# Selective attention and a SwiGLU block in one kernel: two of four head pairs of the second batch transposed by DMA over a DRAM scratch, two on TensorE

## The chip, the cores and the metric

The kernel runs on one core of a Trainium2 chip. A core has TensorE for matrix products, VectorE, ScalarE and GpSimd (POOL in the profile) for elementwise work, SyncE (SP) which here only issues DMAs, and 16 DMA engines that move data between DRAM and the on-chip memory. Each engine takes its instructions in order. Engines wait for each other by semaphores. Products of TensorE land in PSUM, which has eight banks here, and another engine must copy them out.

The metric is the time of one execution on the device in microseconds (us). The time before is the median of six runs.

## The reference

Causal attention with a bias from a running sum, then a gated feed-forward block over all tokens:

```python
scores = scale * np.matmul(q, k.transpose(0, 1, 3, 2))      # q, k, v: (8, 8, 576, 64)
cum = np.cumsum(np.maximum(s, 0.0), axis=-1)
bias = -(cum[:, :, :, None] - cum[:, :, None, :])
scores = np.where(causal, -1000000000.0, scores + np.minimum(bias, 0.0))
attn = softmax(scores)
x = np.matmul(attn, v).transpose(0, 2, 1, 3).reshape(B * S, H * D)   # (4608, 512)
g = x @ w_gate
out = (g * sigmoid(g) * (x @ w_val)) @ w_out                         # d_ff = 1536
```

## The kernel before

There are 64 heads (8 batches of 8), numbered through; head 8 is the first of batch 1. Heads are handled in groups of four for the keys and queries (group 4 is heads 16 to 19) and in pairs for the result (pair 4 is heads 8 and 9, the first pair of batch 1).

**Attention.** For a head, `score_piece` (line 344) makes the scores in four pieces on TensorE (line 367), ScalarE takes the exponential into `pt` (line 380), and POOL masks the diagonal (lines 383 and 388). `av_piece` (line 395) multiplies with the values (line 405); a column of ones gives the sum, and `av_out` divides on VectorE (lines 421 and 422) into `ot`, a tile of 128 tokens by 5 chunks by the 128 columns of a pair. Three `ot` tiles rotate.

**From ot to XT.** The feed-forward block needs x with the columns on the partitions, in `XT`, a ring of three token tiles of 512 tokens. There are two ways. `x_pe` (line 448) transposes the five chunks of a pair on TensorE (line 455) into a PSUM bank, and VectorE copies it to `XT` (line 462; ScalarE in batch 0, line 460). `x_out` (line 438) stores `ot` to a DRAM scratch `XS`, issued by POOL (line 439), and later `x_in` (line 443) has SP issue a transposing DMA from there into `XT` (line 446):

```python
def x_out(pr):
    nc.gpsimd.dma_start(
        XS[pr].rearrange("(c p) d -> p c d", p=128), ots.pop(pr)
    )

def x_in(pr):
    b, r = divmod(pr, H // 2)
    for lo, hi, at in x_parts(b):
        nc.sync.dma_start_transpose(XT[:, r, at : at + hi - lo], XS[pr][lo:hi])
```

Batches 0 and 1 take the first way, batches 2 to 7 the second.

**Keys and queries.** `load_qk` loads a group (line 152, SP), `cast_one` casts it to 16 bit (line 249 on POOL). Groups 0 to 4 are transposed on TensorE: `prep_one` calls `pe_transpose` (line 291) and `pe_out` (lines 318 and 320). From group 5 on (`NPE = 5`) they too go over DRAM: `scratch` stores the casts to `ks` and `qs` (line 263, SP), `transposes` loads them transposed into `pk` and `pq` (line 273, SP), and `split` copies them into `KQ` on VectorE (line 278).

**The order of work.** It is written out by hand. `first_batch` does batch 0. Then nine token tiles of the feed-forward block run (`ffn_items`: gate product line 571, value product line 586, output product line 620), and after each of their 36 items `pump` runs the generator `attn_items` up to a position that grows with the item number. In `attn_items` step kk emits the scores of head kk; `side` adds the loads, casts and scratch transfers of later groups after the second piece, and `PREP_AT` names the places of the TensorE transposes of the keys and queries of groups 3 and 4. After the scores of step kk come, in this order, the transposes named by `X_AT`, and then the products and divisions named by `AV_AT`. For batch 1, step 12 divides heads 8 and 9, step 13 transposes pair 4 and divides heads 10 and 11, step 14 transposes pair 5. The casts of group 4 are emitted at the start of step 13, and the first TensorE transpose of its keys after the fourth score piece of step 13. On SP the loads of group 6 come in step 12, and the scratch stores of group 5 in step 15.

The first token tile of the feed-forward block reads tokens of batch 0 alone; the second, tokens 512 to 1023, reads all four pairs of batch 1 as well.

The lines that choose the way are these three conditions: the set of scratch tiles (line 84), the choice between `x_pe` and `x_in` (line 541), and the call of `x_out` (line 554).

Of the kernel before, what the change touches and what calls it, by code (L numbers as in the profile page):

```python
# [13 lines left out]
BF16 = mybir.dt.bfloat16  # L14
# [5 lines left out]
def kernel(  # L20
# [14 lines left out]
    B, H, S, D = q.shape  # L35
    NT, DM = out.shape
    DF = moe_w_gate.shape[1]
    BH = B * H
    NCH = 5
# [24 lines left out]
    def pt_col(tj, bi):  # L64
# [12 lines left out]
    dram = ctx.enter_context(  # L77
        tc.tile_pool(name="dram", bufs=1, space=bass.MemoryType.DRAM)
    )

    NPE = 5
    XB = 2
    KS = {i: dram.tile([NR * S, 128], BF16, name=f"ks{i}") for i in range(NPE, NHB)}
    XS = {
        i: dram.tile([NCH * 128, 128], BF16, name=f"xs{i}") for i in range(XB * H // 2, BH // 2)
    }
    QS = {i: dram.tile([NR * S, 128], BF16, name=f"qs{i}") for i in range(NPE, NHB)}

# [17 lines left out]
    with tc.manual_schedule():  # L106
# [78 lines left out]
        def aug(hb, engs):  # L185
            for hh in range(HB):
                r, e = divmod(hh, 2)
                r0 = 64 * (1 - r)
                bh = hb * HB + hh
                engs[hh].dma_start(  # L190
                    KQ[hb % 2][r][r0 : r0 + 4, :, e * S : (e + 1) * S],
                    HL[bh : bh + 1, :, :, :],
                )
# [48 lines left out]
        def cast_one(hb, name, eng):  # L242
            cts[name, hb] = cp.tile([128, J, NR, D], BF16, tag="c" + name, bufs=2, name="c" + name)
            dst = cts[name, hb].rearrange("x j r d -> x r j d")
            src_t = loaded[name, hb]
            if eng is nc.scalar:
                nc.scalar.copy(dst, src_t)
            else:
                eng.tensor_copy(dst, src_t)
# [145 lines left out]
        def av_piece(bh, bis):  # L395
            b, h = divmod(bh, H)
            if bis[0] == 0:
                bs = take()
                avs[bh] = (view(bs, NCH * (D + 1)), bs)
            av = avs[bh][0]  # L400
            pt = pts[bh]
            for bi in bis:
                for tj in range(bi + 1):
                    c0 = pt_col(tj, bi)
                    nc.tensor.matmul(  # L405
                        av[:, bi * (D + 1) : (bi + 1) * (D + 1)],
                        pt[:, c0 : c0 + 128],
                        VT[b % 2][:, tj, h, :],
                        start=(tj == 0),
                        stop=(tj == bi),  # L410
                    )

        def av_out(bh):
            pr, e = divmod(bh, 2)
            if e == 0:
                ots[pr] = otp.tile([128, NCH, 2 * D], BF16, tag="ot", name="ot")
            ot = ots[pr]
            av, bs = avs.pop(bh)
            av3 = av.rearrange("p (c e) -> p c e", e=D + 1)
            rc = small.tile([128, NCH], FP32, tag="rc", name="rc")  # L420
            nc.vector.reciprocal(rc, av3[:, :, D])  # L421
            nc.vector.tensor_mul(  # L422
                ot[:, :, e * D : (e + 1) * D],
                av3[:, :, 0:D],
                rc[:, :, None].to_broadcast([128, NCH, D]),
            )
            give(bs)
            pts.pop(bh)
# [9 lines left out]
# [10 lines that stand above are left out]
        def x_pe(pr, eng=None):  # L448
            b, r = divmod(pr, H // 2)
            ot = ots.pop(pr)  # L450
            bs = take()
            ps = view16(bs, S)
            for c in range(NCH):
                n = 128 if c < 4 else TAIL
                nc.tensor.transpose(
                    ps[:, c * 128 : c * 128 + n], ot[0:n, c, :], ident[0:n, 0:n]
                )
            for lo, hi, at in x_parts(b):
                if eng is nc.scalar:
                    nc.scalar.copy(XT[:, r, at : at + hi - lo], ps[:, lo:hi])  # L460
                else:
                    nc.vector.tensor_copy(XT[:, r, at : at + hi - lo], ps[:, lo:hi])
            give(bs)

        def side(h, step):
            bh = HB * h + step
            if bh == H + 3:
                for c in range(5):
                    cast_v(1, c, nc.gpsimd)
            if h >= 3 and h + 3 < NHB and step == 0:  # L470
                load_qk(h + 3)
            if h + 1 < NHB and h + 1 >= NPE:
                if step == 0:
                    transposes(h + 1)
                    aug(h + 1, GP4)
                if step == 2:
                    split(h + 1, "k", nc.vector)
                if step == 3:
                    split(h + 1, "q", nc.vector)
            if h + 2 < NHB and h + 2 >= NPE:  # L480
                if step == 1:
                    cast_one(h + 2, "k", nc.gpsimd)
                if step == 2:
                    cast_one(h + 2, "q", nc.gpsimd)
                if step == 3:
                    scratch(h + 2)
            bn = h // 2 + 1
            if 2 <= bn < B:
                if h % 2 == 0:
                    if step == 2:  # L490
                        load_v(bn, (0, 1))
                    if step == 3:
                        load_v(bn, (2, 3, 4))
                else:
                    if step == 1:
                        cast_v(bn, 0, nc.gpsimd)
                        cast_v(bn, 1, nc.gpsimd)
                    if step == 2:
                        cast_v(bn, 2, nc.gpsimd)
                        cast_v(bn, 3, nc.gpsimd)  # L500
                    if step == 3:
                        cast_v(bn, 4, nc.gpsimd)

        def prep_one(hb, i):
            g, nm = divmod(i, 2)
            nm = ("k", "q")[nm]
            pe_transpose(hb, nm, g)
            for r in range(2):
                pe_out(hb, nm, g, r, nc.scalar if nm == "k" else nc.vector)
# [12 lines left out]
        def attn_items():  # L522
            for kk in range(H, BH + 2):
                h, step = divmod(kk, HB)
                if kk < BH:
                    if step == 1 and 3 < h + 1 < NPE:
                        cast_one(h + 1, "k", nc.gpsimd)
                        cast_one(h + 1, "q", nc.gpsimd)
                    if step == 0 and 3 < h + 1 < NPE:
                        aug(h + 1, GP4)  # L530
                    for ci in range(4):
                        score_piece(kk, ci)
                        if ci == 1:
                            side(h, step)
                        yield kk + 0.1 + ci / 8
                        if (step, ci) in PREP_AT.get(h, ()):
                            prep_one(h + 1, PREP_AT[h][step, ci])
                            yield kk + 0.1 + ci / 8
                for x in X_AT.get(kk, (kk - 2,)):
                    if x % 2 == 1 and H <= x < BH:  # L540
                        if x < XB * H:
                            x_pe(x // 2)
                            yield kk + 0.5
                        else:
                            x_in(x // 2)
                for p in AV_AT.get(kk, (kk - 1,)):
                    if H <= p < BH:
                        av_piece(p, (0, 1, 2))
                        yield kk + 0.6
                        av_piece(p, (3,))  # L550
                        yield kk + 0.7
                        av_piece(p, (4,))
                        av_out(p)
                        if p >= XB * H and p % 2 == 1:
                            x_out(p // 2)
                        yield kk + 0.8

# [159 lines left out]
        first_batch()  # L717
        second_psum()
        at = attn_items()
        state = {"pos": float(H)}  # L720

# [57 lines left out]
```

The softmax here doesn't subtract the row's maximum and nothing guards it: scores larger than these inputs give would overflow.

## Time and profile before

| what | value |
|---|---|
| median of six runs | 389.79 us (388.37 to 390.64) |
| the profiled execution: its time | 390.23 us |
| the profiled execution: span from first to last instruction | 388.5 us |
| granted clock of TensorE, mean | 0.998 |
| DMA queue of SP (q1) | 90816 packets, 45.36 MB, 49.4% of 16 engines |
| DMA queue of POOL (q0) | 9680 packets, 18.32 MB, 17.9% |
| transposes of x on TensorE, line 455 | 40 (20 in batch 0, 20 in batch 1) |
| copies of them on VectorE, line 462 | 4, 452 to 458 ns each |
| stores to `XS`, line 439 | 24, 862 to 951 ns each on POOL, 2.7 to 7.0 us to landing |
| transposing loads from `XS`, line 446 | 32, median 1138 ns each on SP |

The profiled execution's time is longer than its span by 1.7 us, which lie before the first and after the last instruction. The rows of the page give an engine's busy time, the 40 slices show it in tenths over the span, each slice 9.7 us long. In a timeline a row is the start and duration in us, the engine, the line, the operation, and what it writes and reads. An idle time in square brackets names what ended it. A row with SPq is a DMA issued by SP, its duration the time of issuing alone.

### The profile page before, as it was taken

What the parts mean: (1) busy time and instruction counts of PE and PEld (TensorE: products, weight loads), DVE (VectorE), ACT (ScalarE), POOL (GpSimd) and SP (SyncE); (2) the same over time, 40 slices, a digit from 0 to 9 for tenths busy, and PEclk for the clock granted to TensorE, in tenths of its full rate; (3) what the DMA queues carried; (4) which work ended last, traced back from release to release, by engine and by line L of the source; (5) the groups of instructions that cost most, each with busy time, mean ns of one, the idle gap of its engine ahead of it and who ended that gap; (6) DMA issues with size and microseconds to landing.
All of it is one profiled execution on the core that took longest, in us unless ns stands there. A gap on an engine that the chain in (4) does not pass through costs nothing.

```text
span 388.5 us, 7949 instructions
## 1 busy us (share of the span) xinstructions
PE 371.8 (96%) x3006; PEld 206.9 (53%) x3006; DVE 241.6 (62%) x431; ACT 214.4 (55%) x411; POOL 192.9 (50%) x329
## 2 busy tenths in 40 slices
PE   3779999999999999999999999999999999999995
PEld 2666556655555555555555555555555544444443
DVE  7666787458854786369735884588347625733750
ACT  7586787666646565566556555565465513323321
POOL 7584368565795766566656666576342220011001
PEclk9999999999999999999999999999999999999999
DMA  7999999996859998995789758964231222002002
GB/s 242 202 242 262 197 259 255 310 258 163 174 159 249 288 216 220 214 265 153 181 218 278 133 181 142 291 156 98 61 113 35 32 73 68 3 27 81 2 13 96
DMA packets 100535, 64.18 MB, mean 165 GB/s; under 512 B 81889, under 2 KB 85825, under 8 KB 100497
## 3 DMA queue, kind: packets, MB, share of 16 engines
q1 hardware_dynamic: 90816, 45.36, 49.4%
q0 software_dynamic: 9680, 18.32, 17.9%
q8 instruction: 23, 0.38, 0.4%
q14 instruction: 16, 0.12, 0.1%
HBM read 37.90 MB, written 19.86 MB: 149 GB/s over the span
## 4 chain that ended last, share of the span: by engine, by line
PE 82%; DVE 6%; DMA 5%; issue 3%; ACT 2%; POOL 0%; DVEq 0%; ACTq 0%; SPq 0%; POOLq 0%
PE bank L571 21%; PE bank L620 21%; PE bank L586 20%; PE bank L367 9%; PE bank L405 6%; DMA pk<-ks 2%; PE wide L367 2%; DVE pp L578 2%; ACT pt L380 1%; DVE ht L591 1%; DVE kq L320 1%; DMA kq<-HL 1%; PE one L405 1%; DMA XT<-xs 1%; DMA s_sb<-in_s_dram 1%
## 5 line engine op out<-in xcount | busy, mean ns | idle before, releaser
L380 ACT ACTIVATE pt<-bank 128x512 bf16<-128x512 f32 x224 | 104.2, 504 | 40.3 <-PE bank L367 26.6
L578 DVE SCALAR_TENSOR_TENSOR pp<-th,bank 128x512 bf16<-128x512 bf16 x108 | 74.1, 686 | 70.3 <-ACT th L576 69.5
L571 PE MATMUL bank<-XT,wg 128*128 128x512 bf16 x432 | 111.0, 379 | 1.2 <-DMA XT<-xs 0.6
L586 PE MATMUL bank<-XT,wv 128*128 128x512 bf16 x432 | 110.9, 379 | 0.0
L576 ACT ACTIVATE th<-bank 128x512 bf16<-128x512 f32 x108 | 64.5, 597 | 77.6 <-PE bank L571 73.3
L620 PE MATMUL bank<-wo,ht 128*128 128x512 bf16 x420 | 102.4, 379 | 0.0
L591 DVE TENSOR_TENSOR ht<-pp,bank 128x512 bf16<-128x512 bf16 x108 | 74.0, 685 | 8.8
L367 PEld LDWEIGHTS <-kq 128*128 128x128 bf16 x576 | 46.9, 100 | 39.4 <-issue 5.6
L367 PE MATMUL bank<-kq 128*128 128x128 bf16 (+4 forms) x504 | 65.9, 240 | 0.4 <-DVE ht L591 0.2
L383 POOL TENSOR_SCALAR_AFFINE_SELECT pt<-pt 128x512 bf16<-128x512 bf16 x64 | 41.2, 644 | 35.8 <-ACT pt L380 35.2
L571 PEld LDWEIGHTS <-wg 128*128 128x128 bf16 x432 | 38.3, 98 | 36.4 <-issue 1.0
L586 PEld LDWEIGHTS <-wv 128*128 128x128 bf16 x432 | 38.5, 98 | 34.9 <-issue 0.8
L620 PEld LDWEIGHTS <-ht 128*128 128x128 bf16 x420 | 37.1, 98 | 34.4
L405 PEld LDWEIGHTS <-pt 128*128 128x128 bf16 x960 | 41.5, 98 | 20.7
L439 POOL DMA_DIRECT2D xs<-ot x24 | 21.8, 910 | 58.5 <-DVE ot L422 58.5
L634 POOL DMA_DIRECT2D out_dram<-ysb x35 | 19.6, 562 | 60.9 <-ACT ysb L628 60.9
L628 ACT ACTIVATE ysb<-bank 128x512 f32<-128x512 f32 x35 | 20.9, 597 | 40.9 <-PE bank L620 39.8
L405 PE MATMUL bank<-vt,pt 128*128 128x65 bf16 x840 | 42.8, 194 | 0.0
L190 POOL DMA_DIRECT2D kq<-HL x52 | 31.3, 602 | 2.3 <-PE bank L571 1.6
L421 DVE RECIPROCAL rc<-bank 128x5 f32<-128x5 f32 x56 | 10.6, 190 | 34.4 <-PE bank L405 34.4
L422 DVE TENSOR_TENSOR ot<-bank,rc 128x320 bf16<-128x320 f32 x56 | 27.5, 492 | 1.9
L388 POOL TENSOR_SCALAR_AFFINE_SELECT pt<-pt 128x64 bf16<-128x64 bf16 x64 | 16.9, 264 | 21.2 <-ACT pt L380 21.1
(68 smaller groups left out, 213.7 us busy)
## 6 DMA issues: line engine op xcount, KB each, us to landing
out_dram<-ysb POOLq DMA_DIRECT2D x35, 256.0 KB, 3.1
rawk<-in_k_dram SPq DMA_DIRECT2D x15, 576.0 KB
rawq<-in_q_dram SPq DMA_DIRECT2D x15, 576.0 KB
rawv<-in_v_dram SPq DMA_DIRECT2D x32, 256.0 KB
xs<-ot POOLq DMA_DIRECT2D x24, 160.0 KB, 3.7
ks<-ck SPq DMA_DIRECT2D x11, 288.0 KB
qs<-cq SPq DMA_DIRECT2D x11, 288.0 KB
wg<-in_moe_w_gate_dram POOLq DMA_DIRECT2D x2, 768.0 KB, 11.5
```

Source lines behind the costliest of these rows:

```text
L190: engs[hh].dma_start(KQ[hb % 2][r][r0 : r0 + 4, :, e * S : (e + 1) * S], HL[bh : bh + 1, :, :, :],)
L367: nc.tensor.matmul(sc[:, o : o + w], T[:, 1, e * S + 128 * tj : e * S + 128 * (tj + 1)], T[:, 0, e * S + lo : e * S + hi], start=True, sto ...
L380: nc.scalar.activation(pt[:, c0 : c0 + W], sc[:, 0:W], AF.Exp, scale=0.125)
L383: nc.gpsimd.affine_select(pt[:, 1088:1600], pt[:, 1088:1600], pattern=[[0, 4], [1, 128]], compare_op=ALU.is_ge, fill=zreg, base=0, channel ...
L405: nc.tensor.matmul(av[:, bi * (D + 1) : (bi + 1) * (D + 1)], pt[:, c0 : c0 + 128], VT[b % 2][:, tj, h, :], start=(tj == 0), stop=(tj == bi),)
L422: nc.vector.tensor_mul(ot[:, :, e * D : (e + 1) * D], av3[:, :, 0:D], rc[:, :, None].to_broadcast([128, NCH, D]),)
L571: nc.tensor.matmul(pg, WG[j][:, c, f0 : f0 + 128], xt[:, c, :], start=(c == 0), stop=(c == 3),)
L576: nc.scalar.activation(th, pg, AF.Tanh, scale=0.5)
L578: nc.vector.scalar_tensor_tensor(pp, in0=th, scalar=1.0, in1=pg, op0=ALU.add, op1=ALU.mult)
L586: nc.tensor.matmul(pv, WV[j][:, c, f0 : f0 + 128], xt[:, c, :], start=(c == 0), stop=(c == 3),)
L591: nc.vector.tensor_mul(ht, pp, pv)
L620: nc.tensor.matmul(py, hts[ft][:, ts_ * 128 : (ts_ + 1) * 128], WO[ft // WKO][:, ft % WKO, :], start=(ft == 0), stop=(ft == NFT - 1),)
```

## The change

Pairs 4 and 5, the first two of batch 1, get a scratch tile in DRAM and take the way over it; pairs 6 and 7 stay on TensorE. Instead of comparing with a number of batches, the two conditions now ask whether the pair has a scratch tile.

```diff
     NPE = 5
-    XB = 2
     KS = {i: dram.tile([NR * S, 128], BF16, name=f"ks{i}") for i in range(NPE, NHB)}
     XS = {
-        i: dram.tile([NCH * 128, 128], BF16, name=f"xs{i}") for i in range(XB * H // 2, BH // 2)
+        i: dram.tile([NCH * 128, 128], BF16, name=f"xs{i}")
+        for i in (4, 5, *range(8, BH // 2))
     }
...
                     if x % 2 == 1 and H <= x < BH:
-                        if x < XB * H:
+                        if x // 2 not in XS:
                             x_pe(x // 2)
                             yield kk + 0.5
                         else:
                             x_in(x // 2)
...
                         av_piece(p, (4,))
                         av_out(p)
-                        if p >= XB * H and p % 2 == 1:
+                        if p // 2 in XS and p % 2 == 1:
                             x_out(p // 2)
```

The store of a pair is emitted right after the division of its second head, in steps 12 and 13; the transposing load stands where the TensorE transposes stood, in steps 13 and 14, after the scores. Two groups of five transposes, two PSUM banks taken and given back, and two copies on VectorE are gone; two stores on POOL's queue and two transposing loads on SP's queue, each waiting for its store, are new.

## The prediction

> **What bounds the kernel now.** I read the page's busy times and 40 slices first, then the waits of TensorE, then the timeline of the stretch in which the two pairs are transposed, and last the queue of SP there.
>
> ```profile
> PE 371.8 (96%) x3006; PEld 206.9 (53%) x3006; DVE 241.6 (62%) x431; ACT 214.4 (55%) x411; POOL 192.9 (50%) x329
> ...
> PE   3779999999999999999999999999999999999995
> ...
> POOL 7584368565795766566656666576342220011001
> PEclk9999999999999999999999999999999999999999
> DMA  7999999996859998995789758964231222002002
> ```
>
> TensorE is at nine tenths or more from slice 5 to the last but one, at full clock. Its list of waits agrees: between 55 and 100 us it has no wait at all. So what is added to or taken from its queue there should reach the end. The DMA engines are also at nine tenths from slice 2 to 9 (10 to 87 us), and POOL is at seven in slice 7 (58 to 68 us). The change takes work from TensorE and gives it to these two and to SP. In the timeline (start, duration, engine, line) the first of the two moved pairs, pair 4, stands like this:
>
> ```profile
> 58.46 0.65 POOL L383 TENSOR_SCALAR_AFFINE_SELECT pt<-pt 128x512 bf16<-128x512 bf16 x1
> ...
> 59.05 0.24 POOL L388 TENSOR_SCALAR_AFFINE_SELECT pt<-pt 128x64 bf16<-128x64 bf16 x1
> 59.23 1.14 POOL L249 CAST ck<-rawk 128x1152 bf16<-128x1152 f32 x1
> ...
> 60.17 0.49 DVE L422 TENSOR_TENSOR ot<-bank,rc 128x320 bf16<-128x320 f32 x1
> 60.32 1.14 POOL L249 CAST cq<-rawq 128x1152 bf16<-128x1152 f32 x1
> ...
> 61.63 0.48 PEld L291 LDWEIGHTS <-ck 128*128 128x128 bf16 x5
> 61.84 0.44 PE L291 MATMUL bank<-ident,ck 128*128 128x128 bf16 x5
> 62.00 1.13 POOL L249 CAST ck<-rawk 128x1152 bf16<-128x1152 f32 x1
> 62.07 0.46 PEld L455 LDWEIGHTS <-ot 128*128 128x128 bf16 x5
> 62.12 0.52 PE L455 MATMUL bank<-ident,ot 128*128 128x128 bf16 x5
> ...
> 62.57 0.63 PE L405 MATMUL bank<-vt,pt 128*128 128x65 bf16 x15
> ```
>
> The reader is to see two things. Line 455 takes TensorE from 62.12 to 62.57, when the next group starts. And POOL casts the keys of group 4 at 59.23, before VectorE has finished the second head of pair 4 (60.66); TensorE loads that cast at 61.63, 1.26 us after it ends.
>
> **The change, part by part.**
>
> *Removed from TensorE.* Two groups of five transposes. By starts a group costs 0.45 us (62.12 to 62.57; 67.28 to 67.73 for pair 5). The chain of waits gives 0.35 and 0.36, the starts of the weight loads 0.50 (62.07 to 62.57). I take 0.45 each, so **0.90 us gained**, bounds 0.70 and 1.00. Here a rule and the row differ widely: "VectorE: DVE Perf Modes", section "The three transpose paths", prices a 128x128 transpose at 390 ns on TensorE and 1309 ns by DMA, and its rules for kernel authors say to use TensorE where PSUM will do, which speaks against the change. By its 390 ns ten transposes would be 3.9 us, a clear gain. But in the row five are done in 0.45 us, because they run one behind the other in a full queue. The row decides, and it leaves little to gain.
>
> *Removed from VectorE.* Two copies of line 462, about 0.46 us each. VectorE does not set the end there (62% busy), so nothing.
>
> *The order of emission.* The interleaving is driven by positions: item n of the first token tile lets the attention run up to 8 + 0.3217 (n - 6). The change drops two stops, at 13.5 and 14.5. The targets around them are 13.468, 13.790 and 14.433, 14.755, so each stop was passed within one call anyway, and the rest of TensorE's order is unchanged. One PSUM take and give less per pair shifts the names of the banks, not how long each rests; I cost it at nothing.
>
> *Added to POOL: the store of pair 4.* Line 439 is emitted after the second head's division (step 12) and before the casts of group 4 (step 13). POOL runs in order, and it waits there for VectorE's `ot`. The profile has the same store for later batches:
>
> ```profile
> L439 POOL DMA_DIRECT2D xs<-ot x24 | 21.8, 910 | 58.5 <-DVE ot L422 58.5
> ```
>
> It idles 2.4 us on average before each. At 88.02 it starts 0.30 us after `ot` ends (87.23 + 0.49), and at 96.77 again 0.30 after. So in our place: POOL free at 59.29, store starts at 60.66 + 0.30 = 60.96, ends 0.91 later at 61.87, and the cast of group 4's keys runs from about 61.88 to 63.02 instead of 59.23 to 60.37. Queued behind the store are the casts of group 4, the mask of head 13, and the casts of group 5. Who waits: TensorE, with line 291, needs that cast. Its weight load can go at about 63.1 and its first transpose, 0.1 us after, at 63.2 instead of 61.84. **A new wait of 1.36 us on TensorE**, bounds 1.1 and 1.6 by the spread of the store (0.86 to 0.95) and of a handover that no row shows for POOL to TensorE (0.05 to 0.3 us). No queue of ready work hides it: TensorE is in order, and the cover, 1.26 us of distance, is smaller than the 2.65 us that the cast moves.
>
> *What else is behind it on POOL.* The cast of group 4's queries ends at 64.2, wanted by TensorE at 65.45: covered. Head 13's mask ends near 64.8, its second product starts at 69.05. The store of pair 5 (after step 13) finds POOL there at about 67.35, later than `ot` of head 11 (65.28 plus the shift of TensorE): no wait, 0.91 us. The queries of group 5 are cast by 70.0 instead of 67.8. Then POOL's own gaps (1.53 us before 70.66, 1.97 before 75.08) take up the delay.
>
> *Added to SP: two transposing loads, each with a wait for its store.* Line 446 takes 1.14 us (median of 32). They come after the loads of group 6 (SP is through with them at 66.25) and before the scratch stores of group 5, lines 263 and 273:
>
> ```profile
> 66.34 0.41 SPq L263 DMA_DIRECT2D ks<-ck  x1
> 67.85 0.35 SPq L263 DMA_DIRECT2D qs<-cq  x1
> ...
> 72.75 2.12 SPq L273 DMA_TRANSPOSE pk<-ks  x1
> ...
> 84.37 1.21 DVE L278 COPY kq<-pk 64x1152 bf16<-64x1152 bf16 x2
> ```
>
> The store lands 3.7 us after issue in the median (2.7 to 7.0). "DMA: Bandwidth & Descriptors", section "Anatomy of one DMA — SWDGE (gpsimd) path", would make it 2.0 us plus the bytes over 436 GB/s, 2.4 us for 160 KB. By the page pair 5's store is there at 69.8; by the row at 67.35 + 3.7 = 71.05, at worst 74.35. I take the row, as the DMA engines are full in this stretch. Pair 4's is there by 66.25 or little later. So SP issues the second load at 71.05 to 72.2, `ks` and `qs` at 72.3 and 72.7 (about 5 us late), the next raw loads until 74.6, and then waits for `ks`. That took 6.4 us before (66.34 to 72.75) behind a megabyte of fresh loads; I estimate 4 us with the rings emptier: `pk` goes out at 76.3 instead of 72.75. Where VectorE waited for `pk`, it came 5.8 to 7.6 us after its issue (133.52 to 139.32, 229.65 to 237.25). So it lands at 82 to 84, and the split that wants it stands at 84.37 plus the shift. **Just covered: nothing**, and up to 2 us if the store lands late (first rival). SP is level again at 84.82, where it already waited for POOL.
>
> *Arrival of x.* The next token tile first reads the two pairs at 80.85. The second load is issued by 72.2; even 7 us after that is before it. The 147 KB that each pair moves twice are small beside the 64 MB of the kernel.
>
> **Sum.** -0.90 + 1.36 = +0.46 us. On the profiled execution, whose own time is 390.23 us with a span of 388.5, that is a span of 389.0 and a time of 390.7. That execution is 0.44 above the median of the runs, 389.79, so I forecast 389.79 + 0.46 = **390.3 us**. A measurement of this kernel can tell about 0.3%, 1.2 us, from no change; the forecast lies inside that.
>
> **The rivals.** *First: the second wait of SP reaches TensorE, slower.* If pair 5's store takes the longest time seen, 7.0 us, SP is held to 74.35, `pk` goes out near 79.6 and lands at 87.0 by the chain's 7.37 us. The split at 84.8 then waits 2.2 us on VectorE, the split of the queries (89.02) moves with it, and line 367 of head 20 reads its first half at 90.20, only 0.5 us after that half is written. TensorE would lose about 1.8 us more: 392.1 us. For it: DMA full in slices 6 to 9, the small margin. Against it: VectorE waited 3.27 us for `pk` before 120.90 and TensorE did not stop. It decides once pair 5's store lands later than about 72.5.
>
> *Second: POOL's wait does not reach TensorE.* If the cast is ready in time after all, for instance because POOL's spans are rough or the store issues faster than its row, only the gain stays: 389.79 - 0.90 = 388.9 us. For it: later batches have this store before casts and TensorE stays full. Against it: there nothing on TensorE needs POOL's next casts at once, as groups from 5 on go over DRAM; groups up to 4 are transposed on TensorE.
>
> *Third: the change does nothing visible,* as the two paths cancel by chance or the pairs take the old way. The condition puts pairs 4 and 5 into the scratch set, so the old way is excluded; the rest is the forecast itself.
>
> **How the numbers follow.** Forecast 0.50, own range 389.4 to 391.0; first rival 0.30; second 0.15; something unseen 0.05. The forecast gives same 0.46, slower 0.03, faster 0.01. The first rival gives slower 0.28, same 0.02. The second sits 0.9 below, near the bound: same 0.11, faster 0.04. The unseen rest gives 0.03 and 0.02. Together faster 0.08, same 0.59, slower 0.33. The range from 388.8 to 392.3 takes in both rivals' places; a longer chain behind `pk` lies above it.
>
> **What the changed profile would show.** Right: line 455 with ten matmuls instead of twenty in the first token tile; POOL's line 439 near 61 us with an idle of 1.6 us before it; a wait of TensorE's line 291 for POOL's `ck` of 1.1 to 1.6 us near 63 us, the only new one; SP's scratch stores of group 5 at 71 to 74 us. Wrong: no such wait at line 291 (then the second rival), or a wait of line 367 near 90 us after VectorE's `kq` (the first), or of line 571 for `XT` near 81 us, which I have excluded.

## The result and the profile after

The changed kernel takes 391.2 us in the median against 389.84 us for the kernel before on the same chips; the ratio is 1.0031 with a 95% interval of 1.0018 to 1.0045, so 0.7 to 1.8 us slower. The forecast was 0.46 us slower, inside 0.3%; the measured middle, 1.2 us, lies on that bound, and the forecast lies below the interval. Every ratio in this document leaves out executions that ran 5 to 10 us longer at a slightly lower clock: one of the changed kernel, nine of 22 with the store later, three of 22 with pair 5 alone, and one of 22 with pair 5 alone and the raw loads behind. The profiled execution has a span of 389.7 us against 388.5, and its own time is 391.4 against 390.23.

The page of the changed kernel first: busy times, the slices of TensorE, POOL, clock and DMA, and the row of the stores.

```profile
PE 371.2 (95%) x2996; PEld 206.2 (53%) x2996; DVE 240.2 (62%) x429; ACT 214.3 (55%) x411; POOL 194.1 (50%) x331
...
PE   3779998999999999999999999999999999999995
...
POOL 8584368765695756566656666576342220011001
PEclk9999999999999999999999999999999999999999
DMA  7999999896859988893788758965231122002002
...
L439 POOL DMA_DIRECT2D xs<-ot x26 | 23.6, 910 | 63.7 <-DVE ot L422 63.7
```

TensorE has lost its ten transposes (2996 products for 3006) and yet ends later; slice 7, around 63 us, is the one that fell from nine tenths to eight. The clock is unchanged. The timeline there, to be laid beside the one before:

```profile
58.60 0.24 POOL L388 TENSOR_SCALAR_AFFINE_SELECT pt<-pt 128x64 bf16<-128x64 bf16 x1
...
59.91 0.49 DVE L422 TENSOR_TENSOR ot<-bank,rc 128x320 bf16<-128x320 f32 x1
...
60.69 0.94 POOL L439 DMA_DIRECT2D xs<-ot  x1 [1.85 <-DVE ot L422]
...
61.63 1.16 POOL L249 CAST ck<-rawk 128x1152 bf16<-128x1152 f32 x1
...
62.84 0.28 PEld L291 LDWEIGHTS <-ck 128*128 128x128 bf16 x5 [1.59 <-POOL ck L249]
62.85 0.45 PE L291 MATMUL bank<-ident,ck 128*128 128x128 bf16 x5 [1.10 <-DVE ht L591]
```

POOL waits for the second head, stores, and only then casts the keys that TensorE wants. The row of the weight load (PEld) names POOL as what ended its idle time. The product row names VectorE's `ht` instead, which ends at 62.84, almost with the cast (62.79). But in the kernel before these products start at 61.84, ahead of that `ht` at 62.41, so they do not need it. Here the row of the weight load is the one to read.

SP's queue and the split that it must feed:

```profile
72.54 0.53 SPq L263 DMA_DIRECT2D ks<-ck  x1
...
75.52 1.87 SPq L273 DMA_TRANSPOSE pk<-ks  x1
...
84.46 1.21 DVE L278 COPY kq<-pk 64x1152 bf16<-64x1152 bf16 x2
```

The keys of group 5 go out 2.8 us later than before and are still in time: no idle is noted at 84.46. The next group isn't. First the kernel before, then the changed one:

```profile
80.56 0.68 SPq L263 DMA_DIRECT2D ks<-ck  x1
84.82 0.36 SPq L263 DMA_DIRECT2D qs<-cq  x1
...
94.81 2.17 SPq L273 DMA_TRANSPOSE pk<-ks  x1
...
102.20 2.13 DVE L278 COPY kq<-pk 64x1152 bf16<-64x1152 bf16 x2
...
105.70 1.02 PE L586 MATMUL bank<-XT,wv 128*128 128x512 bf16 x4
```

```profile
82.68 3.58 SPq L263 DMA_DIRECT2D ks<-ck  x1
86.31 0.43 SPq L263 DMA_DIRECT2D qs<-cq  x1
...
96.39 1.99 SPq L273 DMA_TRANSPOSE pk<-ks  x1
...
103.95 0.92 DVE L278 COPY kq<-pk 64x1152 bf16<-64x1152 bf16 x2 [1.81 <-DMA pk<-ks]
...
106.25 1.02 PE L586 MATMUL bank<-XT,wv 128*128 128x512 bf16 x4 [0.19 <-DVE pp L578]
```

SP is 1.5 us late at the queries' scratch store of group 6, as the keys' store alone now takes 3.58 us to issue, and it is still 1.6 us late when it sends for the transposed keys. VectorE waits 1.81 us for them, its next work on the feed-forward block comes later, and TensorE, which stood 0.09 us behind the kernel before up to 104 us, is 0.55 us behind at the products of line 586 (106.25 for 105.70).

To see where TensorE's queue falls behind, I matched the rows of lines 578 and 591, which follow each product of the feed-forward block, one by one between two profiled executions. The table gives the change of the distance to the kernel before, in us (plus is later), over three stretches, for all kernels of this study. Neither line has rows from 62 to 80 us, so the state at 78 is read from the first rows of the next token tile. The column at 33 us is the distance at the first product of line 571, which starts at 32.77 us in the kernel before, ahead of the first instruction that any edit touches. The last column is the time against the kernel before, with its interval.

| kernel | at 33 us | 33 to 78 | 78 to 165 | 165 to 380 | ratio of times |
|---|---|---|---|---|---|
| changed | -0.28 | +0.37 | +0.74 | +0.13 | 1.0031 (1.0018 to 1.0045) |
| store later | -0.73 | -0.91 | +0.55 | -0.18 | 1.0018 (1.0000 to 1.0036) |
| loads of x later | +0.01 | +0.36 | +0.37 | -0.05 | 1.0047 (1.0028 to 1.0066) |
| both later | -0.57 | -0.90 | +2.06 | -0.12 | 1.0068 (1.0042 to 1.0093) |
| no transposes | -0.26 | -0.93 | +0.86 | -0.01 | 0.9979 (0.9961 to 0.9997) |
| stores alone | -0.53 | +1.28 | +0.03 | +0.05 | 1.0032 (1.0020 to 1.0045) |
| pair 4 alone | -0.49 | +0.83 | +2.02 | -0.03 | 1.0027 (1.0014 to 1.0041) |
| pair 5 alone | -0.71 | -0.47 | +0.39 | -0.10 | 1.0029 (1.0006 to 1.0053) |
| before, raw loads behind | +0.78 | +0.01 | +0.01 | -0.18 | 0.9989 (0.9976 to 1.0001) |
| changed, raw loads behind | -2.11 | +0.71 | +0.02 | -0.01 | 0.9995 (0.9977 to 1.0014) |
| store later, raw loads behind | -1.23 | -0.91 | +2.23 | -0.03 | 1.0007 (0.9992 to 1.0022) |
| all three orders turned | -2.72 | +2.11 | +0.01 | +0.06 | 0.9995 (0.9974 to 1.0017) |
| pair 5 alone, raw loads behind | -2.40 | 0.00 | +0.63 | +0.07 | 0.9990 (0.9978 to 1.0003) |

For the changed kernel: +0.37 is the wait less the ten transposes, as forecast, and then 0.46 near 104, where the late split sits, and about 0.3 near 144 are lost in the second stretch, which the forecast had at nothing. Each row is one execution, the time is that of many.

The first column matters for what follows. In all executions but one it stands by 19 us, and a large part of it comes from a change of TensorE's pace. The second nine of the score products, first in the kernel before, then with all three orders turned:

```profile
13.70 1.49 PE L367 MATMUL wide<-kq 128*128 128x128 bf16 x9 [0.63 <-ACT pt L380]
```

```profile
12.84 0.95 PE L367 MATMUL wide<-kq 128*128 128x128 bf16 x9 [0.63 <-ACT pt L380]
```

The same nine products take 1.49 us in one and 0.95 in the other, at a granted clock of 1.00 in both; from 19 to 24 us nine score products take 0.95 in every execution. In all five kernels with the raw loads behind, TensorE is 1.2 to 3.5 us ahead at 19 us (the kernel before with that edit loses its 3.5 again by 33 us, 2.8 of them in one wait for cast values), in the other eight at most 0.74. The first DMA that this edit reorders is issued at 68 us in the kernel before. Whether the early start is chance or comes with the edit is not known, so the times of these five cannot be put down to the order of the loads alone.

### The profile page after: what moved, and what is told of

The parts are those of the page before. It is cut to its first block, busy times and chain, and to the rows that moved or that the text cites. A ratio compares the mean times of both kernels' runs of the same rounds, so it can differ in the third digit from the quotient of the medians.

```text
span 389.7 us, 7939 instructions
## 1 busy us (share of the span) xinstructions
PE 371.2 (95%) x2996; PEld 206.2 (53%) x2996; DVE 240.2 (62%) x429; ACT 214.3 (55%) x411; POOL 194.1 (50%) x331
## 4 chain that ended last, share of the span: by engine, by line
PE 78%; DVE 7%; DMA 7%; issue 3%; ACT 2%; SPq 1%; POOL 1%; DVEq 0%; ACTq 0%; POOLq 0%
PE bank L620 21%; PE bank L571 20%; PE bank L586 19%; PE bank L367 8%; PE bank L405 6%; DMA pk<-ks 3%; DVE pp L578 2%; DVE ht L591 2%; PE wide L367 2%; ACT pt L380 1%; DVE kq L278 1%; DMA rawq<-in_q_dram 1%; DVE kq L320 1%; DMA XT<-xs 1%; PE one L405 1%
## 5 line engine op out<-in xcount | busy, mean ns | idle before, releaser
L439 POOL DMA_DIRECT2D xs<-ot x26 | 23.6, 910 | 63.7 <-DVE ot L422 63.7
```

## The experiments

My theory after the result: two losses, POOL's wait at 62 us (1.1 to 1.3 us) and transposed keys that come late through SP (0.7 us), against 0.9 us saved. The rival: the added DMA traffic itself, wherever the instructions stand. In the cuts of code below, `...` marks lines left out.

**What the ten transposes are worth.** Pairs 4 and 5 are left out on their way; their part of `XT` is zeroed.

```diff
-                        else:
+                        elif x // 2 >= 8:
                             x_in(x // 2)
...
-                            x_out(p // 2)
+                            if p // 2 >= 8:
+                                x_out(p // 2)
+                            else:
+                                ots.pop(p // 2)
...
+            1: [lambda: prep_one(2, 0), lambda: nc.gpsimd.memset(XT[:, 0:2, S : 2 * S], 0.0)],
```

> The kernel with pairs 4 and 5 left out on their way to XT: neither transposed nor stored nor loaded, their part of XT is set to zero once, early, on POOL, so their share of the feed-forward block is left out. Theory: what the ten transposes cost TensorE, 0.9 us by the starts of the rows, so 0.8 to 1.0 us below the kernel before and no wait at line 291. Rival (the transposes were hidden behind weight loads or other waits): within 0.3 us of the kernel before.

The time is 0.21% below (0.03 to 0.39%), 0.8 us, and TensorE is ahead by 0.93 us at 78 us: the forecast's 0.90 agrees with both. But its trace also shows how the gain can be lost again without any of the change's DMAs. VectorE's row near 123 us:

```profile
122.14 0.94 DVE L278 COPY kq<-pk 64x1152 bf16<-64x1152 bf16 x2 [5.69 <-DMA pk<-ks]
```

The keys of group 7 are not there sooner because TensorE is, VectorE waits for them, and TensorE is back by about 0.8 us there in this execution. With 389.82 us it is 1.5 us above the median of this kernel, 388.36, so most executions seem to keep more.

**What the stores cost by themselves.** The kernel before, with two stores that nobody reads.

```diff
+                        if p // 2 in (4, 5) and p % 2 == 1:
+                            nc.gpsimd.dma_start(
+                                XS[p // 2].rearrange("(c p) d -> p c d", p=128), ots[p // 2]
+                            )
```

> The kernel before, all transposes of batch 1 still on TensorE, with the two stores to the scratch added on POOL at the places of the change; nothing reads them. Theory (POOL's wait for the second head holds up the cast that TensorE wants): TensorE waits 1.1 to 1.3 us at line 291 near 62 us and the time is 0.9 to 1.5 us (0.25 to 0.4%) above the kernel before. Rival (the loss sits in SP's waits and loads alone): no wait at line 291 and within 0.3 us of the kernel before.

0.32% slower (0.20 to 0.45%), 1.2 us, with the wait in its place, and TensorE loses 1.28 us by 78 us and nothing later:

```profile
60.43 0.94 POOL L555 DMA_DIRECT2D xs<-ot  x1 [1.46 <-DVE ot L422]
...
61.37 1.16 POOL L249 CAST ck<-rawk 128x1152 bf16<-128x1152 f32 x1
...
62.58 0.28 PEld L291 LDWEIGHTS <-ck 128*128 128x128 bf16 x5 [1.59 <-POOL ck L249]
```

That settles the first loss: it comes with the store on POOL, without SP's part.

**Moving either half.** The store of pair 4 behind the casts of group 4 on POOL, the two loads of x behind the scratch stores of group 5 on SP, and both:

```diff
                         cast_one(h + 1, "q", nc.gpsimd)
+                        x_out(4)
...
-                        if p // 2 in XS and p % 2 == 1:
+                        if p // 2 in XS and p % 2 == 1 and p // 2 != 4:
```

```diff
-                        else:
+                        elif x // 2 >= 8:
                             x_in(x // 2)
...
                     scratch(h + 2)
+                    if h + 2 == 5:
+                        x_in(4)
+                        x_in(5)
```

> The changed kernel with the store of pair 4 moved behind the two casts of group 4 on POOL. Theory (two waits: TensorE for POOL's cast near 62 us, 1.1 to 1.3 us, and a later one through SP's queue, about 0.7 us): TensorE's wait at line 291 is gone, the second store of the pair is still late on SP, and the time is 1.1 to 1.3 us (0.3%) below the changed kernel, about level with the kernel before. Rival (the added DMA traffic itself costs the time, wherever the instructions stand): the wait goes but the time stays within 0.4 us of the changed kernel.

> The changed kernel with the two transposing loads of pairs 4 and 5 moved behind the scratch stores of group 5 on SP, the store of pair 4 left where it was. Theory: SP issues the scratch stores of group 5 by about 70 us and the transposing loads of group 6 a microsecond or more sooner than in the changed kernel, TensorE's wait at line 291 stays at 1.1 us, and the time is 0.5 to 0.8 us below the changed kernel. Rival (traffic itself): no gain, within 0.3 us of the changed kernel.

> Both moves: the store of pair 4 behind the casts of group 4, and the two transposing loads behind the scratch stores of group 5. Theory: neither wait is left, only the ten transposes are gone, and the time is 0.7 to 1.0 us (0.2 to 0.25%) below the kernel before. Rival (traffic itself): the time is level with or above the kernel before.

With the store later, the wait at line 291 is gone and TensorE is 0.91 us further at 78 us, but the ratio, 1.0018, is not clearly apart from the changed kernel's. The loads of x later gain nothing in time (1.0047), though in the trace the first half of the expectation came true: SP waits only 0.5 us for a store, the keys of group 6 go out at 95.23 instead of 96.39, VectorE does not wait for them and the 0.46 us near 104 are not lost; 0.37 us are lost near 123 instead. Both together are the worst of the three (1.0068, six executions, three at 390.7 to 391.3 us and three at 392.9 to 393.1), where the theory wanted 0.7 to 1.0 us below the kernel before. Its trace, of an execution of the lower three, shows a part of why that sum fails: TensorE is ahead by 0.90 us at 78 and gives up 1.6 near 104, where VectorE waits for the keys of group 6, and more near 123:

```profile
103.55 0.92 DVE L278 COPY kq<-pk 64x1152 bf16<-64x1152 bf16 x2 [2.96 <-DMA pk<-ks]
...
122.98 0.94 DVE L278 COPY kq<-pk 64x1152 bf16<-64x1152 bf16 x2 [5.20 <-DMA pk<-ks]
```

So moving the loads of x did not make the keys of all the next groups come in time, and the rival, traffic wherever it stands, had forecast the result of both moves. At this point I gave up the theory that SP's wait for the store alone makes the keys late. The test was not clean, though: with both moves SP still waited 2.1 us for the store of pair 5, until 72.26, and sent for the keys of group 5 at 74.65 instead of 72.75. What remained to try was that they stand behind 1.15 MB of raw loads in the queue.

**The raw loads behind.** One order turned in `side`, in the kernel before, in the changed one, and with the store moved as well:

```diff
-            if h >= 3 and h + 3 < NHB and step == 0:
-                load_qk(h + 3)
             if h + 1 < NHB and h + 1 >= NPE:
                 if step == 0:
                     transposes(h + 1)
...
+            if h >= 3 and h + 3 < NHB and step == 0:
+                load_qk(h + 3)
```

> The kernel before with one order turned on SP: the transposing loads of the next group's keys and queries are issued ahead of the raw loads of a later group, not behind them. Theory (TensorE's gains are given back where the transposed keys of groups 6 to 8 land late, near 105, 123 and 143 us, because 1.15 MB of raw loads stand ahead of them): VectorE's waits for the transposed keys, 4.8 us in the kernel before, fall under 1 us, and as TensorE lost only about 0.4 us there, the time is 0 to 0.6 us below the kernel before. Rival (those landings depend on the amount of traffic, not on the order): VectorE's waits stay above 3 us and the time is unchanged.

> The changed kernel with the same order turned on SP. Theory: the wait at line 291 stays (1.1 us), the two later steps back of TensorE (0.46 us near 105, 0.28 near 145) go, so 0.5 to 0.9 us below the changed kernel, 0.2 to 0.6 us above the kernel before. Rival (amount of traffic): within 0.3 us of the changed kernel, VectorE's waits for the transposed keys above 4 us.

> The changed kernel with both cures: the store of pair 4 behind the casts of group 4 on POOL, and the transposing loads of keys and queries ahead of the raw loads on SP. Theory: neither the wait at line 291 nor the later steps back are left, only the ten transposes are gone, 0.7 to 1.2 us (0.2 to 0.3%) below the kernel before. Rival (amount of traffic): level with the kernel before or above it.

In the changed kernel the loss in time is gone: 0.9995 (0.9977 to 1.0014) against 1.0031 (1.0018 to 1.0045), intervals that do not meet, 1.4 us. Its profiled execution has no wait of VectorE for keys left (7.2 us in four waits before the edit) and no loss after 78 us, where the changed kernel loses 0.87, while the wait at line 291 stands. That is what the order of the loads can have done. But this execution also began the first token tile 1.83 us sooner than the changed kernel's, and lost 0.34 us more than it by 78 us. So how much of the 1.4 us is the order's is not shown. The row of the wait among the waits of TensorE (total, times, longest):

```profile
PE bank L291 <- POOL ck L249: 1.5, 1, 1.5
```

The kernel before gains 0.11% by the same edit, not clear of nothing (0.9989, 0.9976 to 1.0001), and in its trace nothing changes between 33 and 165 us: its 4.8 us of such waits were covered.

The third kernel is a miss. With POOL's wait cured too it should have been 0.7 to 1.2 us below the kernel before, and it is level (1.0007). In its trace TensorE is 0.91 ahead at 78 us and gives up 1.16 by 85 and 1.2 near 123:

```profile
83.67 0.92 DVE L278 COPY kq<-pk 64x1152 bf16<-64x1152 bf16 x2 [1.37 <-DMA pk<-ks]
```

```profile
PE bank L572 <- DMA XT<-xs: 1.1, 1, 1.1
```

The first is the forecast's first rival itself, at group 5: the loads of x held SP until 74.8 us, and the keys went out at 78.07. The second is a landing of x for the next token tile that TensorE, ahead until then, has to wait for.

**One pair at a time,** by taking 4 or 5 out of the set of scratch tiles:

```diff
-        for i in (4, 5, *range(8, BH // 2))
+        for i in (5, *range(8, BH // 2))
```

> The changed kernel with pair 4 alone over the scratch, pair 5 back on TensorE. Theory: pair 4 carries the wait of POOL: TensorE waits 1.1 to 1.3 us at line 291 and saves only 0.45 us, so 0.5 to 1.2 us (0.15 to 0.3%) above the kernel before. Rival (the loss comes with the number of transfers, half of it with each pair): 0.4 to 0.7 us above the kernel before and no more than for pair 5 alone.

> The changed kernel with pair 5 alone over the scratch, pair 4 back on TensorE. Theory: no wait at line 291; 0.45 us saved on TensorE, part or all of it given back where transposed keys land late, so 0.5 us below to 0.4 us above the kernel before. Rival (half of the loss with each pair): 0.4 to 0.7 us above the kernel before.

Pair 4 alone has the wait at line 291 and costs 0.27%, as expected; its trace is of the slowest of its 22 executions (393.05 us), so the 2.02 us lost there after 78 need not be typical. Pair 5 alone has no such wait, as expected. Its ratio, 1.0029, is outside what the theory gave (up to 0.4 us) and above the rival's half. But three of the 19 executions behind it, at 393.7 to 394.9 us, carry it: the median of the 19 is 389.94 us against 389.66, 0.07%. In its trace SP waited for the store until 70.95 and sent `ks` at 72.27, as late as in the changed kernel, and VectorE waited for keys at every group from 5 to 8, yet TensorE lost no more by all this (0.39 us) than it had gained (0.47). So late keys need only the last of the two pairs; that they cost time in most executions there is not shown.

> Pair 5 alone over the scratch, with the transposing loads of keys and queries ahead of the raw loads. Theory: no wait at line 291 and none for late keys, so the 0.45 us of five transposes stay: 0.3 to 0.8 us below the kernel before. Rival (the gain is given back to the DMA engines whatever the order): level with the kernel before or above it.

With the raw loads behind, pair 5 alone goes from 1.0029 (1.0006 to 1.0053) to 0.9990 (0.9978 to 1.0003), and VectorE waits for no keys. The traces do not show that this was the cause: from 33 us on this execution lost 0.70 us, where the one without the edit gained 0.18, and it began 1.69 us sooner. The gain that the theory wanted below the kernel before, 0.3 to 0.8 us, lies within that interval and is not shown.

> The changed kernel with three orders turned: the store of pair 4 behind the casts of group 4 on POOL, the two transposing loads of x behind the scratch stores of group 5, and the transposing loads of keys and queries ahead of the raw loads. Theory: no wait at line 291, VectorE's waits for transposed keys under 1 us, the second pair's x there before 80 us, so 0.5 to 1.0 us below the kernel before. Rival (TensorE's gain of 0.9 us is always given back to the DMA engines, whatever the order): level with the kernel before within 0.3 us, or above it.

All three orders turned: level with the kernel before (0.9995, 0.9974 to 1.0017), where 0.5 to 1.0 us were expected. In its profiled execution TensorE began the first token tile 2.72 us early and lost 2.11 us of that by the second tile, partly waiting for POOL's casts (0.5 us at line 291, 0.5 at line 405) and most of all for x, the sign that the forecast had excluded (the gate product is on line 575 of this kernel):

```profile
80.45 0.81 PE L575 MATMUL bank<-XT,wg 128*128 128x512 bf16 x3 [1.19 <-DMA XT<-xs]
```

The loads of x, behind the scratch stores, held SP until 76.58 us, and the expectation that x is there before 80 us failed. With so early a start, this execution says nothing about the three orders alone.

## Why the prediction was right, and where it was not

**The transposes, 0.90 us gained:** 0.93 us in the trace without them, 0.8 us in the time (0.1 to 1.5). The price taken from five back-to-back rows held, and the 390 ns each of the Trainium skill ("VectorE: DVE Perf Modes", section "The three transpose paths") would have been four times too much.

**POOL's wait, 1.36 us:** the stores alone cost 1.28 us in the trace and 1.2 us in time. The store started at 60.69 (forecast 60.96, with all of TensorE a quarter microsecond early in this execution), the cast at 61.63, the weight load at 62.84. Store, cast and handover each came within 0.1 us.

**The first stretch of SP:** second load of x at 71.32 us (forecast 71.05), `ks` at 72.54 (72.3), `pk` at 75.52 (76.3), the split in time. The store of pair 5 took 4.5 us to land, nearer the row's 3.7 than the 2.4 worked out from the Trainium skill ("DMA: Bandwidth & Descriptors", section "Anatomy of one DMA — SWDGE (gpsimd) path").

**Arrival of x at 80.85:** no wait at line 571 there in the changed kernel. Right.

**What failed: "SP is level again at 84.82".** It was at 86.31. In the kernel before SP had waited there for POOL's cast, from 81.24 to 84.82, and the forecast counted on this wait to take up the delay. But SP came 2.12 us late and the scratch store itself took 2.90 us longer to issue (3.58 for 0.68), 5.0 us together and more than the 3.6 us of room. The lateness went on to group 6, and TensorE lost 0.46 us near 104 and about 0.3 near 144. This term was put at nothing; with it the sum is 0.46 + 0.74 = 1.2 us, the measured size.

How firm is that? It is read from one execution. By times alone, stores and missing transposes make 1.2 - 0.8 = 0.4 us, and the changed kernel's 1.2 leaves 0.8, but the intervals of the three are 1.0 to 1.4 us wide, so this rest is not clear of noise. The fit to 1.2 may be partly luck.

The first rival had the mechanism, but placed it at group 5 only, and priced it at 1.8 us more; by its own sign, a store of pair 5 that lands after 72.5, it did not come true (71.3). I checked the first consumer behind the shifted queue and not the next two. Whether the late keys would vanish with SP's waits for the stores, as I then believed, is open: both moves left 2.1 us of these waits, and with the loads of x later alone (0.5 us left) the keys of group 6 came in time and those of group 7 did not. That they vanish when the raw loads stand behind is shown in five traces but for one wait of 1.37 us; what this is worth in time is not, because of the early starts.

Two readings of the slices are one off: POOL is at eight tenths, not seven, in slice 7, and TensorE is at nine from slice 4. No term rests on them.

**The second rival,** that POOL's wait does not reach TensorE, is out: it is in every profile that has the store there.

What stays open: why the kernels with POOL's wait cured end no earlier than those with it, once the raw loads stand behind (1.0007 and 0.9995). Their profiled executions name other late landings, of x near 80 and 123 us and of keys near 84, but each is one execution, and each had begun early. That TensorE, whenever it is ahead, runs into transfers that come no sooner, until about 145 us, fits these rows; it was not tested by taking traffic away, and the kernel without the transposes, 0.8 us faster, shows that a gain is not always lost.

## What to carry to other kernels

Before a DMA is issued from an engine that also computes, look at what that engine does next and who waits for it: 0.9 us of issuing cost 1.3 us on another engine, since it also waited for its data. When a queue is delayed, follow the delay past its first consumer until a wait of the old trace has more room than the delay; covered once is not covered for good. A microsecond saved on the engine that sets the end can be lost again at the next transfer that comes no sooner; look for it in the trace. And compare where two executions stand before the edit acts: here a shift of up to 2.7 us, larger than every difference in time found, was there already.

## What was not expected of the hardware

The first token tile began between 2.72 us earlier and 0.78 us later than in the kernel before, with the same instructions ahead of it, and a good part of that stayed to the end. A large part of it is one change of TensorE's pace, from 1.49 to 0.95 us for nine products, which came between 10 and 19 us and which the granted clock, 1.00 throughout this stretch in the two executions compared, does not show. And issuing a scratch store from SP, 0.68 us at 80.56 in the kernel before, took 3.58 us at 82.68 in the changed one. The DMA engines were at nine tenths in that slice in both, so that alone does not explain it.
